# The last row tile of the output computed and stored in three column pieces instead of two

## The chip, the core and the metric

The kernel runs on one core of a Trainium2 chip. The metric is the device time of one execution in microseconds, as the median of a few runs. The span in the profile is one such execution from its first to its last recorded instruction. It is 1.7 to 2.1 us shorter than the device time of that execution.

The profile calls TensorE PE, VectorE DVE, ScalarE ACT and SyncE SP. ACT and SP also issue DMAs, which are the transfers to and from memory. PSUM is the memory that the matmuls write to, SBUF the one from which the stores read. A semaphore is a counter by which a waiting engine learns that something is finished. A store has "landed" when its semaphore has its last count.

## The reference

The reference is an attention with a sliding window and a few global tokens, followed by a feed-forward block. Only its second half matters here:

```python
attn_out = _attn_ref(q, k, v, global_idx)             # 8 x 8 heads x 576 x 64
x = attn_out.transpose(0, 2, 1, 3).reshape(4608, 512)
h = x @ w_in                                           # 512 -> 2048
g = np.maximum(h, 0.0) ** 2
out = g @ w_out                                        # 2048 -> 512, fp32, 4608 rows
```

## The kernel before

The output has 36 row tiles of 128 rows. For each, TensorE accumulates 16 matmuls over the 2048 inner columns in one PSUM bank, DVE copies the bank to SBUF, and a DMA stores it. The last row tile is already treated apart: it is computed in two halves of 256 columns, so that the first half is copied and stored while TensorE works on the second. What bears on the change:

```python
def expert_bank():
    banks["n"] += 1
    return pst("tr" if banks["n"] % 4 == 0 else "mm", [P, 512])

def store(c, m, cols, po, queue):
    w = cols.stop - cols.start
    ot = sbt("ot", [P, dm], FP32, bufs=4)
    dve.tensor_copy(out=ot[:, 0:w], in_=po[:, 0:w])
    r0 = c * TC + m * P
    queue.dma_start(out=out[r0 : r0 + P, cols], in_=ot[:, 0:w])

def last_rows_out(c, m):
    for i, cols in enumerate((slice(0, dm // 2), slice(dm // 2, dm))):
        po = expert_bank()
        for f in range(NFF):
            nc.tensor.matmul(
                po[:, 0 : dm // 2], gts[c][:, f, m * P : (m + 1) * P], w_out[:, f, cols],
                start=(f == 0), stop=(f == NFF - 1),
            )
        store(c, m, cols, po, nc.sync if i == 0 else act)

def mm2(c, m, part):
    # ... the last tile goes to last_rows_out ...
    for f in range(part * 4, part * 4 + 4):
        nc.tensor.matmul(
            po, gts[c][:, f, m * P : (m + 1) * P], w_out[:, f, :],
            start=(f == 0), stop=(f == NFF - 1),
        )
    if part == 3:
        store(c, m, slice(0, dm), po, nc.sync)
```

The softmax here doesn't subtract the row's maximum and nothing guards it: scores larger than these inputs give would overflow.

## Time and profile before

| | before |
|---|---|
| device time, median of 3 | 326.37 us (326.36 to 327.01) |
| span of the profiled run | 326.0 us (that run took 327.83 us and is not one of the three) |
| TensorE busy | 97% |
| first matmul of the last row tile | 319.14 us |
| last copy out of PSUM starts | 322.83 us |
| last store issued | 323.29 us |
| its landing seen by SP | 325.05 us |

From the first matmul on, the rows are read as a relay. The matmuls end, the copy starts, the copy ends, the store is issued, and then no engine works while the bytes travel and are confirmed. What a change to the last tile can be worth is the length of these steps. The prediction shows the lines of the profile they are from.

Two rows tell which engine issues the stores and how long an issue lasts (columns: how many, shortest, median and longest ns, starts of the first and the last). They are from the view of the output tile between 318 and 326 us in the kernel before:

```profile
L566 SPq DMA_DIRECT2D out_dram<-ot x2: 332/332/332, 320.1 to 321.5; - x2
...
L566 ACTq DMA_DIRECT2D out_dram<-ot x1: 377/377/377, 323.3 to 323.3; - x1
```

The reader is to see that the very last store goes through ACT, and that its issue is 45 ns longer than SP's.

### The profile page before, as it was taken

To read this page: it belongs to the slowest core of one execution; us is meant where nothing else is said; L and a number is where in the kernel's file an instruction comes from. 1 tells how busy PE (TensorE), PEld (TensorE's weight loads), DVE (VectorE), ACT (ScalarE), POOL (GpSimd) and SP (SyncE) were. 2 spreads that over 40 slices of the span, in tenths; PEclk is the share of its full clock that TensorE was granted. 3 is DMA by queue.
4 is the path that set the end of the run, shared out by engine and by line. 5 is a ranking of instruction groups with operands and counts; after the bars stand their busy time and mean duration, and the time that the engine had idled before them with its cause. 6 is when DMAs were issued, how large, how long until landed. Compare 5 with 4: busy or idle time off the path is not lost.

```text
span 326.0 us, 6920 instructions
## 1 busy us (share of the span) xinstructions
PE 316.8 (97%) x2434; PEld 164.5 (50%) x2434; DVE 227.0 (70%) x674; ACT 214.4 (66%) x418; POOL 110.2 (34%) x148
## 2 busy tenths in 40 slices
PE   6998999999999999999999999999999999999996
PEld 2645775445555455455545544454455544444444
DVE  7786987677878875987598758885888675313421
ACT  6677985569954995499549954995499636404600
POOL 9824663639800870089107700680000000000000
PEclk9999999999999999999999999999999999999999
DMA  8999999999994999399959996999610011011012
GB/s 186 176 204 190 174 186 167 154 147 107 153 131 141 73 138 171 134 83 139 132 162 82 148 126 144 98 134 132 139 60 0 34 58 39 2 73 56 2 54 75
DMA packets 148229, 37.53 MB, mean 115 GB/s; under 512 B 136171, under 2 KB 143715, under 8 KB 148195
## 3 DMA queue, kind: packets, MB, share of 16 engines
q0 software_dynamic: 105168, 17.93, 78.9%
q1 hardware_dynamic: 42880, 19.04, 30.3%
q8 instruction: 19, 0.31, 0.4%
q10 hardware_dynamic: 146, 0.13, 0.1%
q14 instruction: 16, 0.12, 0.1%
HBM read 37.30 MB, written 17.05 MB: 167 GB/s over the span
## 4 chain that ended last, share of the span: by engine, by line
PE 88%; DVE 7%; ACT 2%; issue 1%; DMA 1%
PE mm L587 29%; PE mm L524 26%; PE tr L524 9%; PE tr L587 7%; PE sc L679 3%; PE acc L679 3%; PE sc L627 3%; PE mm L543 2%; PE acc L627 2%; DVE xT L751 2%; PE tr L197 1%; DVE vb L457 1%; PE sc L670 1%; DVE xT L732 1%; ACT rec L702 1%
## 5 line engine op out<-in xcount | busy, mean ns | idle before, releaser
L587 PE MATMUL mm<-w_out,gt 128*128 128x512 f16 x448 | 104.4, 379 | 0.0
L524 PE MATMUL mm<-xT,w_in 128*128 128x512 f16 x384 | 90.8, 379 | 0.5 <-DVE xT L751 0.5
L587 PEld LDWEIGHTS <-gt 128*128 128x128 f16 x560 | 52.4, 98 | 58.6
L524 PEld LDWEIGHTS <-w_in 128*128 128x128 f16 x512 | 47.5, 98 | 53.7 <-issue 0.8
L529 ACT ACTIVATE rl<-mm 128x512 f16<-128x512 f32 x96 | 54.3, 599 | 26.7 <-PE mm L524 26.7
L530 DVE TENSOR_TENSOR gt<-rl 128x512 f16<-128x512 f16 x128 | 51.0, 422 | 17.0 <-ACT rl L529 15.6
L636 ACT ACTIVATE et<-sc 128x880 f16<-128x880 f32 (+1 forms) x32 | 29.0, 907 | 44.1 <-PE sc L627 39.1
L643 DVE TENSOR_TENSOR et<-et,mask 128x880 f16<-128x880 f16 (+1 forms) x64 | 38.9, 615 | 24.1 <-ACT et L636 23.8
L113 POOL DMA_DIRECT2D vb<-in_v_dram x40 | 40.7, 1532 | 9.0 <-DMA w_in<-in_moe_w_in_dram 7.3
L524 PE MATMUL tr<-xT,w_in 128*128 128x512 f16 x128 | 33.0, 380 | 0.0
L564 DVE COPY ot<-mm 128x512 f32<-128x512 f32 (+1 forms) x29 | 19.7, 680 | 18.0 <-PE mm L587 16.3
L636 ACT ACTIVATE et<-acc 128x880 f16<-128x880 f32 (+1 forms) x32 | 29.1, 909 | 1.0 <-PE acc L627 1.0
L703 ACT ACTIVATE rec<-rec 128x288 f32<-128x288 f32 x64 | 28.3, 443 | 2.0
L732 DVE TENSOR_TENSOR xT<-sc,rec 64x288 f16<-64x288 f32 (+1 forms) x55 | 25.0, 455 | 6.5 <-ACT rec L703 6.2
L732 DVE TENSOR_TENSOR xT<-acc,rec 64x288 f16<-64x288 f32 (+1 forms) x55 | 25.0, 455 | 3.9 <-ACT rec L703 1.1
L404 POOL DMA_DIRECT2D scr_k<-in_k_dram x30 | 26.6, 1111 | 2.8 <-issue 2.8
L679 PEld LDWEIGHTS <-vb 128*128 128x128 f16 x288 | 21.3, 98 | 11.5
L930 POOL COPY pin<-gsh 1x1 f32<-1x1 f32 x5 | 0.9, 177 | 76.4 <-DVE gsh L720 76.4
L702 ACT ACTIVATE rec<-sc 64x288 f32<-64x288 f32 (+1 forms) x55 | 22.3, 406 | 6.2 <-PE sc L679 4.2
L404 POOL DMA_DIRECT2D scr_q<-in_q_dram x24 | 25.1, 1585 | 3.0 <-DMA w_out<-in_moe_w_out_dram 3.0
L587 PE MATMUL tr<-w_out,gt 128*128 128x512 f16 x112 | 25.3, 379 | 0.0
L702 ACT ACTIVATE rec<-acc 64x288 f32<-64x288 f32 (+1 forms) x55 | 22.2, 404 | 2.0 <-PE acc L670 1.1
(147 smaller groups left out, 308.5 us busy)
## 6 DMA issues: line engine op xcount, KB each, us to landing
out_dram<-ot SPq DMA_DIRECT2D x35, 256.0 KB
vb<-in_v_dram POOLq DMA_DIRECT2D x32, 120.0 KB, 11.3
scr_q<-in_q_dram POOLq DMA_DIRECT2D x24, 144.0 KB, 5.9
scr_k<-in_k_dram POOLq DMA_DIRECT2D x24, 120.0 KB, 4.2
w_in<-in_moe_w_in_dram POOLq DMA_DIRECT2D x4, 512.0 KB, 11.9
w_out<-in_moe_w_out_dram POOLq DMA_DIRECT2D x4, 512.0 KB, 12.3
natk<-in_k_dram POOLq DMA_DIRECT2D x3, 288.0 KB, 10.9
natq<-in_q_dram POOLq DMA_DIRECT2D x3, 288.0 KB, 15.8
```

What stands on the lines that cost most here:

```text
L113: pool.dma_start(out=vb[b][NG : NG + KN[x], x, 2 * hs.start : 2 * hs.stop : 2], in_=v[b, hs, x * KT : x * KT + KN[x]].rearrange("h s d -> ...
L404: pool.dma_start(out=scr[(nm, b % 2)][x * pitch + off : x * pitch + off + hi - lo].rearrange("s (h d) -> s h d", d=D), in_=src[nm][b, :, l ...
L524: nc.tensor.matmul(ph, w_in[:, t, u * P : (u + 1) * P], xT[:, t, XOFF + c * TC : XOFF + (c + 1) * TC], start=(t == 0), stop=(t == NDM - 1),)
L529: nc.scalar.activation(out=rl, in_=ph, func=AF.Relu)
L530: nc.vector.tensor_tensor(out=gts[c][:, u, :], in0=rl, in1=rl, op=ALU.mult)
L587: nc.tensor.matmul(po, gts[c][:, f, m * P : (m + 1) * P], w_out[:, f, :], start=(f == 0), stop=(f == NFF - 1),)
L636: act.activation(out=et[:, :, 0:W], in_=sc[:, :, 0:W], func=AF.Exp, bias=0.0, scale=scale)
L643: dve.tensor_tensor(out=et[:, :, 0:W], in0=et[:, :, 0:W], in1=mask[:, MB[half] : MB[half] + W].unsqueeze(1).to_broadcast((P, 2, W)), op=AL ...
L679: nc.tensor.matmul(banks[e][:, o : o + w], vtf[:, t, vo : vo + P], et[:, e, so : so + w], start=(n == 0), stop=(n == nw - 1), skip_group_c ...
L702: act.activation(out=rec[r], in_=av[xs][rs, :, 0:GTOK], func=AF.Ln)
L703: act.activation(out=rec, in_=rec, func=AF.Exp, scale=-1.0)
L732: dve.tensor_tensor(out=xT[r, hp, x0 : x0 + HS].rearrange("p (k x) -> p k x", k=2), in0=av[x][r, :, 0:GTOK], in1=rec[r], op=ALU.mult,)
```

## The change

The intent is to make the last piece smaller, because only its copy and its store lie behind the last matmul. The second half becomes two pieces of 128 columns; the middle piece is stored through ACT and the last one through SP.

```diff
     def last_rows_out(c, m):
-        for i, cols in enumerate((slice(0, dm // 2), slice(dm // 2, dm))):
+        for i, cols in enumerate((slice(0, 256), slice(256, 384), slice(384, dm))):
             po = expert_bank()
             for f in range(NFF):
                 nc.tensor.matmul(
-                    po[:, 0 : dm // 2], gts[c][:, f, m * P : (m + 1) * P], w_out[:, f, cols],
+                    po[:, 0 : cols.stop - cols.start], gts[c][:, f, m * P : (m + 1) * P], w_out[:, f, cols],
                     start=(f == 0), stop=(f == NFF - 1),
                 )
-            store(c, m, cols, po, nc.sync if i == 0 else act)
+            store(c, m, cols, po, act if i == 1 else nc.sync)
```

## The prediction

> **What bounds the kernel now.** I read the page first: busy shares, the chain that ended last, and the 40 slices, to learn which engine sets the end and whether the change touches it.
>
> ```profile
> span 326.0 us, 6920 instructions
> PE 316.8 (97%) x2434; PEld 164.5 (50%) x2434; DVE 227.0 (70%) x674; ACT 214.4 (66%) x418; POOL 110.2 (34%) x148
> ...
> PE 88%; DVE 7%; ACT 2%; issue 1%; DMA 1%
> ```
>
> The kernel is bound by TensorE from end to end: it is busy 97% of the span and carries 88% of the chain. The change leaves all of that alone and rewrites only the last 128 output rows, so what it can win or lose lies in the last few microseconds. I then asked for the chain and the timeline of that stretch. The columns are start, length and what ran.
>
> ```profile
> 308.94 10.36 PE mm L587 x48
> 319.30 1.75 PE tr L572 x16
> 321.05 1.76 PE mm L572 x16
> 322.81 0.02 issue
> 322.83 0.42 DVE ot L564
> ```
>
> ```profile
> 319.14 1.91 PE L572 MATMUL tr<-w_out,gt 128*128 128x256 f16 x16
> 320.88 1.91 PE L572 MATMUL mm<-w_out,gt 128*128 128x256 f16 x16
> 321.08 0.42 DVE L564 COPY ot<-tr 128x256 f32<-128x256 f32 x1 [1.05 <-PE tr L572]
> 322.83 0.42 DVE L564 COPY ot<-mm 128x256 f32<-128x256 f32 x1 [1.32 <-PE mm L572]
> 323.29 0.38 ACTq L566 DMA_DIRECT2D out_dram<-ot  x1
> ```
>
> The reader is to see a strict relay: 16 matmuls of the first half (1.75 us), 16 of the second (1.76 us), the copy of the second half out of PSUM (0.42 us), its store issued on ACT at 323.29, and then nothing on any compute engine until 326.0. That empty 2.7 us is the store itself and the end of the program. The waits of the SP queue split it:
>
> ```profile
> SPq L967 <- DMA out_dram<-ot: 1.8, 1, 1.8
> ```
>
> SP, which closes the program, waits 1.8 us for the last store to land, from 323.29 to about 325.05. Some 1.0 us of closing semaphores and drains follow to 326.0; these exist in any version. When the last store moves its bytes is shown by the DMA view of 323.2 to 325.1 (40 slices of 0.0475 us, busy tenths):
>
> ```profile
> DMA  0000000000000000000047999998620000000000
> ```
>
> Bytes flow in slices 20 to 30, from about 324.15 to 324.7, or 0.52 us with the edges. The other 1.25 us or so are 0.86 us from the start of the issue to the first byte and 0.4 us from the last byte to the semaphore. The same view of 319.9 to 322.3 (slices of 0.06 us), for the preceding full-width store of 256 KB:
>
> ```profile
> DMA  0000000000000000679998998896300000000000
> ```
>
> That is 13 slices, 0.78 us: twice the bytes cost 0.26 us more.
>
> **What the Trainium skill says.** (1) "TensorE: Matmul & The Clock Gate", section "Back-to-back issue gap", gives N/2.4 + 2.5 ns for a matmul of N columns by itself at full clock, but for a sustained stream of weight load plus matmul about 81 ns at N=128 (and about 131 ns at N=512). This trace agrees with the formula and contradicts the 512 figure: 10.36 us over 48 matmuls of 512 is 216 ns, and 1.75 over 16 of 256 is 109 ns, each with its own weight load. Whether 128 columns take 56 or 81 ns is the one real dispute here. (2) "VectorE: DVE Perf Modes", section on the TRN2 errata, gives a copy out of PSUM as (120 + FD) cycles at 0.96 GHz for fp32, so 1.04 ns per column. The trace has 691 ns at 512 columns and 423 at 256: 1.047 ns per column, agreeing in slope, with a larger constant. (3) "DMA: Bandwidth & Descriptors", section "Anatomy of one DMA — SWDGE (gpsimd) path", puts about 2.0 us of fixed cost on a DMA, most of it the write receipt. The stores here go another way (hardware queues), and the trace has 1.75 us from issue to semaphore including 0.5 us of bytes: smaller, but likewise mostly fixed, and its larger part lies before the first byte. (4) The same page, "Specifications", gives 512 B as the smallest transfer for line rate. A row of a 128-column fp32 piece is exactly 512 B; no store of the kernel before has that packet, so no run here shows it yet.
>
> **The change part by part.** The first half (256 columns, SP queue) stays as it is. The second half becomes two pieces of 128 columns with a PSUM bank, a copy and a store each; the middle piece's store goes to ACT and the last one's to SP. Added are 16 matmuls, 16 weight loads, one copy and one DMA issue.
>
> Matmuls. From 216 ns at 512 and 109.4 at 256, a column costs 0.416 ns and a matmul 3 ns; 128 columns then take 56.2 ns. Two pieces are 32 x 56.2 = 1.80 us where 16 x 109.4 = 1.75 stood: +0.05 us for streaming the same columns with twice the matmuls. The last matmul starts 0.10 later, since its own slot is shorter, but its own latency falls from 272 ns to about 220 (by the mean 213 of the 112-column and 223 of the 136-column matmuls of the value product): net +0.05 at the start of the last copy, 322.88.
>
> Can the weights keep up? The attention output shows it, where six matmuls with 128x128 weights each (112, 192 and 136 columns, twice) run between expert matmuls:
>
> ```profile
> 260.91 0.55 PE L679 MATMUL acc<-et,vb 128*128 128x112 f16 x6
> 261.29 1.03 PE L587 MATMUL mm<-w_out,gt 128*128 128x512 f16 x4
> ```
>
> From 260.91 to 261.29 is 0.38 us for 880 columns. My two terms give 880 x 0.416 + 6 x 3 = 384 ns: no time for the six loads, although they come at 63 ns each. So a 56 ns pace looks free.
>
> Last copy: 423 - 128 x 1.047 = 289 ns, so -0.13 us.
>
> Last issue: SP takes 332 ns for a store where ACT took 377. SP's first half store was issued at 321.54, and its wait shows it landed near 323.23, 1.69 us later, against 1.75 for ACT with the same bytes. So -0.05 us from the queue.
>
> Bytes: 64 KB in place of 128 KB. The slope of the two DMA views (0.26 us per 128 KB) gives -0.13; I take -0.10, because packets of 512 B should carry some fixed cost that halving does not remove.
>
> Sum on the path: +0.05 - 0.13 - 0.05 - 0.10 = -0.23 us. The middle piece is hidden: its copy would run about 321.98 to 322.27, its issue 322.30, its landing near 324.0, a microsecond before the last. DVE is idle between those copies, the banks of the second and third pieces were emptied by 316.6, and the first half's bytes are through by 322.9.
>
> **The rivals.** First, the weight loads (or the issue of twice as many instructions) bind at 128 columns: 81 ns by the skill's sustained figure makes 32 x 81 = 2.59 us, +0.84 on TensorE and +0.6 in all, so 326.95. For it: 32 such pairs in a row are a longer run than the six above, and loads are recorded as 98 ns long. Against it: those six, and the fact that 98 ns loads already fit under shorter matmuls. I give it about 8%. Second, the tail is only latency: the bytes were never what the wait consisted of, and 512 B packets cost about as much each as 1 KB ones, so the store gains nothing and only the copy and the queue count: -0.10 to -0.15. About 25%. Third, a new wait: SP must issue the last store and only then walk through its closing waits, about seven at 0.06 us, or the last store waits for a queue slot to come free. The first ends near 323.95, well before the landing at about 324.8; the second would wait on a store landed by 323.23, a few hundredths later than the copy. Both near nothing, at worst +0.1. Fourth, the three stores meet in the DMA engines: by the times above they come at 322.4, 323.2 and 324.05, each about half a microsecond long, so they do not.
>
> **Range and chances.** 326.37 - 0.23 = 326.14 us. The mechanism's own spread is about 0.1 either way; the three runs before spread from 326.36 to 327.01, larger than the effect, so the range is mostly that of a median of few runs: 325.85 to 326.60. A change of 2% is 6.5 us, about the whole of what follows the start of the last row tile (319.14 to 326.0), so faster by 2% is practically excluded; slower by 2% would take something that this working does not contain.
>
> **What the changed profile would show.** Two groups of 16 matmuls of 128 columns, starting near 320.88 and 321.78, at 56 ns pace (0.90 us each in the chain). A last copy near 322.88 of 0.29 us. The last issue on SP near 323.20. A last landing near 324.8 and an end near 325.8 in the profile's own span, where the kernel before has 326.0. The 128-column groups taking 1.3 us each would make the first rival right; a last store that still takes 1.7 us from issue to landing would make the second right; a gap between the last copy and its issue would show the third. A difference of more than half a microsecond that is not in the last 7 us would mean that the rest of the program was laid out differently, which I do not expect.

## The result and the profile after

The changed kernel took 326.12 us (median of four runs, 325.86 to 326.49). The kernel before, in the same four rounds, took 326.60 (326.36 to 327.01). The ratio is 0.9985 with a 95% interval of 0.9968 to 1.0002. (A ratio is the mean time of one kernel's fast runs over that of the other's of the same rounds, so it is not quite the ratio of the medians quoted.)

The changed kernel's profiled run has a span of 324.5 us where that of the kernel before has 326.0. That is 1.58 us with the records' own digits, far more than the change can do. The profiled execution of the kernel before was also a long one: 327.83 us, above all its timed runs of these rounds. So the first question is where it comes from. TensorE's timeline of the first microseconds, before and then after:

```profile
6.57 0.64 PE L466 MATMUL mm<-identity,nat0k 96*128 96x96 f16 x6
```

```profile
5.57 0.60 PE L466 MATMUL mm<-identity,nat0k 96*128 96x96 f16 x6
```

These are the same instructions, 300 us ahead of the change, and one run was already 1.0 us earlier than the other. The kernel before lists a wait in that stretch which the changed kernel's list of the same stretch does not have among its ten longest, for the load of the global indices:

```profile
DVE g32c L217 <- DMA g<-in_global_idx_dram: 0.8, 1, 0.8
```

This is a difference between two executions, not between two kernels: the kernel before alone has spans from 324.8 to 326.0 us in its executions. In the eleven profiles of kernels whose last row tile is preceded by the same program, the last row tile starts anywhere from 317.86 to 319.26 us. Therefore all tails below are measured from the first matmul of the last row tile, where runs agree to about 0.01 us.

The end of the chain in the changed kernel (start, length, what ran):

```profile
307.70 10.36 PE mm L587 x48
318.06 1.75 PE tr L572 x16
319.80 1.80 PE mm L572 x32
321.61 0.02 issue
321.63 0.29 DVE ot L564
```

The same 1.75 us for the first half as before, then 32 matmuls of 128 columns in 1.80 us where 16 of 256 took 1.76, and a copy of 0.29 in place of 0.42. The timeline adds the middle piece:

```profile
320.74 0.29 DVE L564 COPY ot<-mm 128x128 f32<-128x128 f32 x1 [0.47 <-PE mm L572]
321.06 0.38 ACTq L566 DMA_DIRECT2D out_dram<-ot  x1
321.63 0.29 DVE L564 COPY ot<-mm 128x128 f32<-128x128 f32 x1 [0.60 <-PE mm L572]
```

The reader is to see that DVE waited 0.60 us for TensorE before the last copy: the middle copy was over in time and is off the path. The bytes of the two last stores, in the DMA view from 322.0 to 323.9 us (40 slices of 0.0475 us, busy tenths):

```profile
DMA  9996300000000000359996300000000000000000
```

The first group is the end of the middle store, the second the last store. They do not touch, and the last one fills 7 slices, where the 128 KB store of the kernel before fills 10 in the same view (the prediction counts 11, with one whose digit rounds to 0).

SP's longest wait for a store is now short, which needs care in reading:

```profile
SPq L967 <- DMA out_dram<-ot: 0.7, 1, 0.7
```

It was 1.8 us before. The store did not become 1.1 us quicker: SP now issues the last store itself and walks through other closing waits before it comes to this one, so only the rest of the store's time is listed as a wait. The store has to be measured from its issue. These are the starts of SP's semaphore instructions that follow the last landing, the kernel before (window 325.0 to 325.09) and the changed one (323.4 to 323.6):

```profile
L967 SPq EVENT_SEMAPHORE  x1: 28/28/28, 325.1 to 325.1; - x1
```

```profile
L967 SPq EVENT_SEMAPHORE  x1: 28/28/28, 323.5 to 323.5; - x1
```

With the instruction records' own three digits, from the first matmul of the last row tile (us; "closing" is from the landing seen by SP to the end of the span):

| kernel | last copy starts | copy | issue starts | landing seen | issue to landing | closing | end |
|---|---|---|---|---|---|---|---|
| before | 3.693 | 0.423 | 4.149 | 5.913 | 1.764 | 0.998 | 6.911 |
| changed | 3.734 | 0.293 | 4.055 | 5.632 | 1.577 | 0.938 | 6.570 |
| difference | +0.041 | -0.130 | -0.094 | -0.281 | -0.187 | -0.060 | -0.341 |

The tail is 0.34 us shorter. The times of whole runs fit that (a ratio of 0.9985 would be 0.49 us), but they do not show it: the interval includes 1.

### The profile page after: what moved, and what is told of

It reads as the page before. It is cut to its first block, busy times and chain, and to the rows that moved or that the text cites. A ratio compares the mean times of both kernels' runs of the same rounds, so it can differ in the third digit from the quotient of the medians.

```text
span 324.5 us, 6956 instructions
## 1 busy us (share of the span) xinstructions
PE 316.8 (98%) x2450; PEld 164.7 (51%) x2450; DVE 226.9 (70%) x675; ACT 214.5 (66%) x418; POOL 110.0 (34%) x148
## 4 chain that ended last, share of the span: by engine, by line
PE 89%; DVE 7%; ACT 2%; issue 1%
PE mm L587 29%; PE mm L524 26%; PE tr L524 9%; PE tr L587 7%; PE sc L679 3%; PE acc L679 3%; PE sc L627 3%; PE mm L543 2%; PE acc L627 2%; DVE xT L751 2%; PE tr L197 1%; PE sc L670 1%; DVE xT L732 1%; PE acc L670 1%; ACT rec L702 1%
```

## The experiments

All of them change the tail, except one that repeats the new matmul form through the whole program. Times in the text are from the first matmul of the last row tile unless it says otherwise. Runs of one execution of the kernel show granted clocks of 0.998 to 1.000. They are compared by the tail and not by their time.

**Only the queue.** Two halves as before, both stores on SP.

```diff
-            store(c, m, cols, po, nc.sync if i == 0 else act)
+            store(c, m, cols, po, nc.sync)
```

> The kernel before with one thing changed: the second half's store (256 columns) goes to SP in place of ACT. All times are taken from the start of the first matmul of the last row tile, to leave out what happens earlier: the kernel before ends 6.91 us after it, the changed one 6.57. Theory (the 0.34 us come from a copy that is 0.13 shorter, a store that is 0.19 quicker from issue to semaphore, about 0.05 of that by the SP queue, and 0.06 of closing work, less 0.04 on TensorE): issue to semaphore falls from 1.76 to about 1.70, and the end comes 6.80 to 6.87 after the start. Rival (the gain is the queue, the pieces do nothing): the end comes at 6.6 already. Rival (the queue does nothing, all of the store's gain is its size): 1.76 and 6.91 stay.

Measured: issue to landing 1.722 in place of 1.764, end 6.868 in place of 6.911; last copy and closing unchanged. So the move away from ACT is worth 0.04 us, and the pieces are worth the other 0.30. Both rivals are out. (No run has three pieces all on SP, so whether the middle store needs ACT is not tested.)

**The queues swapped.** The changed kernel with the middle store on SP and the last on ACT. The way the edit was written also gives the first piece's store to ACT.

```diff
-            store(c, m, cols, po, act if i == 1 else nc.sync)
+            store(c, m, cols, po, nc.sync if i == 1 else act)
```

> The changed kernel with the two 128-column stores swapped: the middle one on SP, the last one on ACT. Theory: the last issue takes 377 ns again and issue to semaphore goes from 1.58 to about 1.63; the order of the closing waits changes too, so the end comes at 6.60 to 6.68 after the start of the last row tile instead of 6.57. Rival (the queue does nothing): 6.57 within 0.02. Rival (the queue is most of it): 6.75 or more.

Measured: the last issue on ACT took 338 ns and not 377, issue to landing 1.587, end 6.582. That is 0.012 from the changed kernel: the theory's 6.60 to 6.68 is missed and the rival's "within 0.02" fits. But ACT's first issue in this run took 372 ns. The gain of the run before could thus be that of avoiding ACT's first store in a long while, and not of avoiding ACT.

**ACT for the last store alone.** The first and middle stores on SP, so the last is ACT's only one.

```diff
-            store(c, m, cols, po, act if i == 1 else nc.sync)
+            store(c, m, cols, po, act if i == 2 else nc.sync)
```

> The changed kernel with the first and middle store on SP and the last on ACT, as ACT's only store. In the swap before, ACT had also been given the first store, by the way the edit was written; its first issue took 372 ns, its second 338, and the end came as with SP. Theory A (ACT's first store after a long time costs some 40 ns more, ACT as such nothing): the last issue takes 372 to 378 ns, issue to semaphore about 1.62, end near 6.61. Theory B (the queue makes no difference once the piece is 128 columns wide): issue 338, issue to semaphore 1.58 to 1.59, end 6.57 to 6.59.

Measured: issue 378 ns, issue to landing 1.617, end 6.612. This is theory A to a hundredth. The row of its timeline, then that of the run before, where the two ACT issues are merged into one row:

```profile
322.88 0.38 ACTq L566 DMA_DIRECT2D out_dram<-ot  x1
```

```profile
320.77 1.99 ACTq L566 DMA_DIRECT2D out_dram<-ot  x2
```

The last ACT store of the second trace began at 322.42 (4.056 after the start of the tile), so its issue lasted 1.99 - 1.65 = 0.34 us. Issue and landing moved together: the first store from ACT, which here had last issued a DMA at the start of the program, took 40 ns more to issue and landed 30 ns later than the second one (1.617 against 1.587), and 40 ns later than SP's. The second one was seen once. Why the first one costs more, no run shows.

**The bytes.** The changed kernel, but the last store moves 4 of its 128 columns. The result is wrong (124 columns of the last 128 rows are never written).

```diff
+        if cols.stop == dm and w == P:
+            w, cols = 4, slice(cols.start, cols.start + 4)
         queue.dma_start(out=out[r0 : r0 + P, cols], in_=ot[:, 0:w])
```

> The changed kernel, but the last store moves only 4 of its 128 columns: 128 packets of 16 B in place of 512 B (the result is wrong on purpose in 124 columns of 128 rows). It tells whether the last store's wait has bytes in it that a smaller piece could still save. Theory (about 1.2 us from issue to semaphore is latency, about 0.35 is the packets being moved, and the packets are part count, part bytes): issue to semaphore falls from 1.58 to 1.35 to 1.48. Rival (bytes hardly matter at this size, packets cost the same each): 1.55 or more. Rival (all of it is bytes): 1.25 or less.

Measured: issue to landing 1.414 in place of 1.577, end 6.404. Theory holds. The packets show why; each row of a store is one packet, eight per DMA engine (mean time of one, from the packet records): 16 B 8.6 ns, 512 B 27.7, 1 KB 47.4, 2 KB 86.4. That is about 8.5 ns plus 0.038 ns a byte. The landings, all from SP with nothing in their way, go 1.414, 1.577, 1.722 and, for the whole tile below, 2.024 us. Some 1.4 us of a store is not bytes: in this run 0.83 us from issue to the first packet, 0.19 us for the packets, 0.38 us from the last packet to the last landing, and the rest until SP sees it.

**No split at all.** The last row tile in one piece of 512 columns, stored by SP.

```diff
-        for i, cols in enumerate((slice(0, dm // 2), slice(dm // 2, dm))):
+        for i, cols in enumerate((slice(0, dm),)):
...
-                    po[:, 0 : dm // 2], gts[c][:, f, m * P : (m + 1) * P], w_out[:, f, cols],
+                    po, gts[c][:, f, m * P : (m + 1) * P], w_out[:, f, cols],
```

> The last row tile in one piece of 512 columns, one copy, one store on SP of 2 KB packets: what splitting is worth at all. Theory: last copy at about 15 x 0.216 + 0.38 + 0.03 = 3.65; copy 0.69; issue at 4.37; issue to semaphore 2.0, as for the other full tiles; closing 1.0; end at 7.36, so 0.49 later than two halves on SP and 0.79 later than the changed kernel. Rival (only the number of pieces or queues matters, the sizes do not): no such steps; 6.9 to 7.0.

Measured: last copy at 3.654, copy 0.691, issue at 4.373, issue to landing 2.024, end 7.456. The steps of the relay came as expected and the end 0.10 later. Of that, 0.06 is the closing, which took 1.059, and most of the rest is the store: two closing waits of SP, 0.06 each, follow the one for the last landing. One followed it in the kernel before (0.998) and none in the changed kernel (0.938). So the 0.06 us of closing that the change won is that the last landing is now the last thing SP waits for. The eleven profiles with this program ahead of the tail all fit that count.

**Smaller still: 256, 192 and 64 columns.**

```diff
-(slice(0, 256), slice(256, 384), slice(384, dm))
+(slice(0, 256), slice(256, 448), slice(448, dm))
```

> The changed kernel with pieces of 256, 192 and 64 columns, so the last copy has 64 columns and the last store 128 packets of 256 B. Times from the first matmul of the last row tile, as before; the changed kernel ends at 6.57. Theory (every part of the relay is linear in the columns of the last piece): the same number of matmuls and columns puts the last copy at 3.73 again; the copy takes 291 - 67 = 224 ns; issue to semaphore, 1.41 with 16 B, 1.58 with 512 B and 1.72 with 1 KB packets, comes to about 1.50; end near 6.42. Rivals: 64-column matmuls do not keep their pace of 30 ns because the weight loads bind (copy later than 3.80), or packets of 256 B cost as much as those of 512 B or the 96 KB of the middle piece are in their way (1.58 or more): end at 6.50 or later.

Measured: last copy at 3.734, copy 0.225, issue at 3.987, but issue to landing 1.629, end 6.554. TensorE kept its pace (29 ns per matmul of 64 columns, each with its own weights), so the first rival is out. The store gave the copy's gain back, as the second rival said. Its packets were small and quick (19.0 ns), and the last one was through 0.10 us sooner than in the changed kernel, yet it was confirmed only 0.46 us after its last packet, where the changed kernel's took 0.39. In the DMA view of this run (322.5 to 325.0 us, slices of 0.0625 us) the middle and the last store form one group:

```profile
DMA  5899984000000000000015999999610000000000
```

**The middle piece out of the way: 320, 128 and 64 columns.** It tells the two readings of the last run apart. Five rounds.

```diff
-(slice(0, 256), slice(256, 384), slice(384, dm))
+(slice(0, 320), slice(320, 448), slice(448, dm))
```

> Pieces of 320, 128 and 64 columns, queues as in the changed kernel. With 256, 192 and 64 the bytes of the last store were through 0.10 earlier than in the changed kernel (5.14 against 5.23 after the start of the last row tile), but its landing came at 5.60 against 5.62: 0.46 after its last byte in place of 0.39. Either rows of 256 B take longer to be confirmed, or the middle store, whose bytes ended at 5.02 and which landed at 5.44, stood in the way. Here the middle piece is 128 columns again and about 0.2 earlier relative to the last. Theory A (the middle store was in the way): bytes through at 5.14, landing near 5.52, end near 6.46. Theory B (rows of 256 B take longer): landing at 5.60, end at 6.54 to 6.56. In the total time, A would be 0.1 under the changed kernel and 0.45 under the kernel before, 0.14%, and five rounds may just show the latter.

Measured: last copy at 3.735, copy 0.225, issue at 3.987, issue to landing 1.478, end 6.403. The bytes of the middle store ended at 4.83, when those of the last began, and the last landed 0.36 us after its last packet. In the DMA view of this run (321.8 to 324.3 us, slices of 0.0625 us) the middle and the last store now have a dip between them:

```profile
DMA  0000000037999997410026985238830000000000
```

Theory A holds, and the end is even 0.06 sooner than it said, because both the packets and the confirmation were quicker. B falls: rows of 256 B are not slower to be confirmed. What held up the last store of the run before was the middle piece of 96 KB, whose packets ran on until 5.02 beside those of the last one. One more thing had differed: there ACT's issue (3.658 to 4.035) overlapped SP's, which began at 3.987. But the last store's first packet came at 4.826 in both runs, so that overlap cost nothing. This is the shortest tail, 0.51 under the kernel before and 0.17 under the changed one. In total time it was 326.79 us (326.58 to 327.62) against 327.25 for the kernel before in the same rounds, a ratio of 0.9989 (0.9975 to 1.0003): the tail is shorter by its trace, and the time doesn't show it.

**Two pieces of 384 and 128 columns**, both on SP.

```diff
-(slice(0, 256), slice(256, 384), slice(384, dm))
+(slice(0, 384), slice(384, dm))
-            store(c, m, cols, po, act if i == 1 else nc.sync)
+            store(c, m, cols, po, nc.sync)
```

> Two pieces only, of 384 and 128 columns, both on SP: the middle piece of the changed kernel is joined to the first. Theory (only the last piece's copy and store are on the path, and each further piece costs 16 matmuls' constant, 0.04 to 0.05): last copy at about 3.69 in place of 3.73, everything after it as in the changed kernel, end near 6.53; the closing waits may be paired otherwise, 6.59 then. Rival (the middle piece is needed, since a copy and store of 384 columns run late and stand in the way of the last ones): 6.7 or more.

Measured: last copy at 3.694, as expected 0.04 sooner than with three pieces. Issue to landing was 1.601, since the 192 KB of the first store had its packets under way until 4.90 while those of the last began at 4.86; closing 0.998, one wait more behind the landing; end 6.614. So 0.04 was won and 0.08 given back, and the third piece is worth having, for reasons other than TensorE's. The number fits neither of the two expected ends to the hundredth and lies just above the theory's second one; the rival's 6.7 is not reached.

**The pace of 128 columns in the long run.** The kernel before with all the other 35 row tiles computed in matmuls of 128 columns. Three rounds. The 81 ns of the rival is the sustained figure that the prediction cites.

```diff
-        for f in range(part * 4, part * 4 + 4):
-            nc.tensor.matmul(
-                po, gts[c][:, f, m * P : (m + 1) * P], w_out[:, f, :],
-                start=(f == 0), stop=(f == NFF - 1),
-            )
+        for s in range(4):
+            for f in range(part * 4, part * 4 + 4):
+                nc.tensor.matmul(
+                    po[:, ts(s, P)], gts[c][:, f, m * P : (m + 1) * P], w_out[:, f, ts(s, P)],
+                    start=(f == 0 and s == 0), stop=(f == NFF - 1), skip_group_check=True,
+                )
```

> The kernel before, with all of the other 35 row tiles of the second product computed in matmuls of 128 columns, four where one of 512 stood, each with its own weight load: 2240 in place of 560, and long runs of them back to back. Copies, stores and the last tile stay as before. The last tile of the changed kernel showed a pace of 55.8 ns over 31 gaps. Theory (the pace is columns over clock plus a small constant, however long the run): 4 x 55.8 = 223 against 216 ns, so 560 x 7.4 ns = +4 us, 4 to 5 with what the other engines make of it: about 331. Rival (weight loads or instruction issue bind once the queue ahead of the array is used up; the 32 in the last tile were too few to show it): 81 ns each, so 560 x 108 ns = +60 us, about 387; anything over 340 speaks for it.

Measured: 334.52 us (334.45 to 335.04) against 327.30 in the same rounds, ratio 1.0223 (1.0206 to 1.0240): +7.2 us. The rival's +60 is out. A run of 192 such matmuls without a break, from its chain:

```profile
315.80 10.72 PE mm L588 x192
```

That is 55.8 ns each, the same as the 32 of the changed kernel; 48 matmuls of 512 columns took 10.36. This makes 560 x 7.4 ns = 4.1 us of the 7.2. The rest shows as idle time ahead of these matmuls, of which the 512-wide ones' row had 0.0 us. Weight loads, then matmuls (busy time, mean ns of one, idle time before them):

```profile
L588 PEld LDWEIGHTS <-gt 128*128 128x128 f16 x2240 | 126.7, 98 | 6.2 <-issue 2.9
L588 PE MATMUL mm<-w_out,gt 128*128 128x128 f16 x1792 | 108.7, 219 | 1.4 <-issue 1.2
```

"Issue" is idle time for which the profile shows no wait. In the records there are seven places where one of these matmuls starts 358 to 609 ns after another instead of 56; together they lose 2.97 us, and 4.1 + 3.0 is the whole. Their cause is open. The program has 32 instruction transfers of 16 KB where the kernel before has 19, which suggests that instructions came late. The packet records don't support it: no instruction transfer is under way during any of the seven. None of it is seen in the last tile.

**The changed kernel again**, unaltered, five rounds on the chip of the run with 320, 128 and 64 columns.

> The changed kernel once more, unaltered, with more rounds and on the chip of the run above: the tail's 0.34 us is 0.10% of the time. Theory: a ratio of 0.9990, interval reaching from about 0.998 to 1.000; the tail again 6.57. Rival (the first measurement's 0.5 us was real and part of it comes from elsewhere in the program): ratio 0.9985 or less with an interval that excludes 0.999.

Measured: 326.72 us (326.63 to 326.92) against 327.25 (327.07 to 327.62), ratio 0.9984 (0.9970 to 0.9998); the tail is 6.564. The interval excludes 1 this time. It doesn't decide between 0.9990, the tail alone, and 0.9985, tail and something else: both lie inside. The kernel with the still shorter tail came out at 0.9989 on the same chip, so a tenth of a per cent is what these rounds can't resolve.

## Why the prediction was right

The forecast of 326.14 us (measured 326.12) was right, but the last digits agree by luck: it was a step of -0.23 from a median of 326.37, and the kernel before came to 326.60 in the rounds that counted. The terms, by the trace:

| term | predicted | measured | how it was told |
|---|---|---|---|
| last copy starts later | +0.05 | +0.041 | the two traces; 32 matmuls at 55.8 ns, last one 219 ns long |
| shorter copy | -0.13 | -0.130 | the two traces |
| queue | -0.05 | -0.042 | both halves on SP |
| fewer bytes | -0.10 | -0.145 | 1.577 against 1.722, both on SP |
| closing | none | -0.060 | waits behind the last landing, counted in each trace |
| sum | -0.23 | -0.341 | with 0.005 between copy and issue |

The matmul and copy terms were right, and so was the choice of the pace: the line through the trace's 216 and 109.4 ns gave 56.2, its six short matmuls said that the loads keep up, and the run has 55.8. Even 2240 of them keep it between their gaps. The first rival was given 8%, and it fell.

The queue term had the right size and half a wrong reason. It was put down to SP against ACT. The swap shows ACT within 0.012 us once it has issued another store shortly before; what cost 40 ns was ACT's first store. (Its 1.69 against 1.75 us were read from rounded waits; the records have 1.708 and 1.764.)

The bytes were under-sized because I expected packets of 512 B to carry a fixed cost that halving doesn't remove. The slope of the two DMA views that I had read, -0.13, was the better guide: a packet's constant is 8.5 ns out of 28 and is paid by the larger packets too, so it cancels. The views' slices had also rounded that slope down: in the packet records the two stores take 0.52 and 0.82 us, so 0.30 per 128 KB and not 0.26, which gives -0.15. The second rival, that the bytes were no part of the wait, is refuted by the store of 4 columns.

Two things were missed. The closing was taken as a constant, "in any version"; it depends on how many of SP's waits stand behind the last landing. And I wrote that a difference above half a microsecond outside the tail would mean a program laid out differently. The profiles differed by 1.24 us there, with TensorE's same instructions at the start of both: single executions of this program vary by that much. The third and fourth rivals (a new wait, stores that meet) came to nothing in the changed kernel, as argued; the pieces of 192 and of 384 columns show that meeting stores do cost when the middle one is large.

## What to carry to other kernels

At the end of this program, which is bound by TensorE, only the last piece's copy and store are exposed, and 1.4 us of that store stayed even with rows of 16 B. So cut the last piece until the next-to-last store is about to run into it, and compare such changes from a landmark near the end of the trace: the start of the program varies by more than the tail can give. Add up the relay step by step, since a wait listed for a queue grows or shrinks with what that queue does ahead of it.

## What the Trainium skill lacked or had wrong

- "TensorE: Matmul & The Clock Gate", "Back-to-back issue gap": its sustained figures for weight load and matmul in a stream, about 81 ns at 128 columns and 131 at 512, do not hold here: 55.8 ns over 192 in a row, and 216. Its formula for a matmul by itself, N/2.4 + 2.5, fits both, and 29 ns at 64 columns, with a load of 128x128 weights ahead of every matmul.
- "DMA: Bandwidth & Descriptors", "Anatomy of one DMA — SWDGE (gpsimd) path": 2.0 us of fixed cost for the GpSimd path. For DMAs from SP or ACT the page's "Specifications" has a first-byte latency of about 0.6 us, but the page does not split what follows. Here a store with 16 B rows took 1.41 us: 0.83 from the start of the issue to the first packet (0.50 from the end of the issue), 0.19 of packets, 0.38 to the last landing.
- The same page, "Specifications": 512 B as the least transfer for line rate. Packets of 256 B took 17.9 to 19.0 ns and 512 B 27.7, near one line (8.5 ns + 0.038 ns a byte) with those up to 2 KB; the runs show no step at 512 B for stores to HBM.
- No page says that the first store issued from ACT, some 320 us after its last DMA, takes longer: 372 to 381 ns to issue, against 338 ns for its next one (seen once), and 30 to 40 ns later landed.
- No page says what a program's own closing waits cost ("Runtime: NRT & Kernel Launch" has times only for what the runtime puts around a kernel): 0.94 us from the last landing seen to the end, plus 0.06 us for each of SP's waits that stands behind it (0.998 with one, 1.059 with two).
